# Output projection of a gated attention layer: tiles 8 and 9 as a fifth pair of seven half products

## The chip, the cores and the metric

The kernel runs on one core of one Trainium2 chip. Its time is the device time of one execution in microseconds (us); lower is better. The core has five engines with a queue of instructions each, which meet at semaphores: TensorE (PE; its weight loads are listed apart as PEld), VectorE (DVE), ScalarE (ACT), GpSimd (POOL) and SyncE (SP), which here issues the transfers.

## The reference, cut to what matters

With S = 2048 rows, D = 640 columns, 32 heads of 20 and F = 1536, all in fp32:

```
xn  = layernorm(x)
q, k, v = split(xn @ wqkv)                  # 32 heads of 20
o   = softmax(q . k[pos - 0,2,..,14]) @ v   # each position sees 8 positions, 2 apart
s   = o @ wo                                # the output projection
h   = (xn @ w_gate) * (xn @ w_up)
g   = silu(h @ w_down)
out = x + s * g
```

The change is in `s = o @ wo`, a product of 2048 x 640 by 640 x 640, and touches the preparation of w_down that runs beside it.

## The kernel before, in words

The rows lie in 16 tiles of 128 (s = 0 to 15). Each fp32 operand of a product is split into a high part, a rounded copy (ScalarE), and a low part, the rest (a subtraction on VectorE or GpSimd). A product is three sweeps of matmuls into one PSUM bank: high by high, high by low, low by high (`ALL3`). The stages run one after the other on TensorE: projections, gate and up; then the output projection; then the down projection, whose products of halves and sums of w_down's blocks need prepared weights ("down weights"). The whole order is written out by hand: each engine executes its instructions in the order in which the Python code issues them.

In the output projection, tiles 0 to 7 are taken in four pairs (p = 0 to 3, `pair_product`), each by seven products of halves after Strassen and Winograd, 320 columns wide: products 0 to 2 have 6 matmuls and products 3 to 6 have 9, as the fifth block of 128 rows of wo is added there in the plain way (`FIFTH`). Products 0, 2, 4 and 6 share bank A, 1 and 3 share bank C, 5 has bank B. ScalarE copies products 0 to 2 out (line 782), VectorE adds the kept ones to products 3, 4 and 5 (lines 785, 788, 790), ScalarE copies product 6 (line 793). Product 4 is read by VectorE before product 6 adds to the same bank.

The operands of a pair come in three parts, each with a high copy (`hi_pair`, line 754, ScalarE) and a low part (`lo_pair`, line 758, VectorE): part 0 is A11, A12 and the fifth block of the first tile, part 1 is S3, A22 and the fifth block of the second, part 2 is the sums S1, S2, S4. `turn_pair` transposes the two tiles (line 481) and forms the sums (734 to 737), after `load_pair` has brought them from DRAM. Product 0 of the next pair is issued ahead of product 6 of this one.

Tiles 8 to 15 go singly (`out_proj`): two halves of 15 matmuls each (line 96), their operand transposed by `turn_o` and split by `split_o`. The first half of tile 8 takes the place that product 0 of a next pair has.

Beside this run the twelve steps of the down weights, two for each k = 0 to 5: `wd_sums` issues their sums on VectorE (T1 and T2, lines 557 and 558; T3 and T4, lines 562 and 563), `wd_splits` their high copies on ScalarE (line 86) and low parts on GpSimd (line 87). T1 and T2 are tiles with the tag "lg", of which there are two buffers; T4 has one ("e"). In the first three pairs one step is taken, in pair 3 two (n = 2), beside each single tile one. In each pair the sums stand ahead of product 1, the splits behind product 4.

Buffers: the tag "wf" has four, two of which hold the first two blocks of wo during this stage. Odd pairs put part 2 into two "wf" buffers. The other parts lie in rows of down weight buffers that are not filled yet (`blocks(y, r, h, n)`: from row r of buffer y): `wd_kv["T4"]`, `wd_kv["B22"]`, `wd_big[0]` to `wd_big[3]`. A tile that is allocated when no buffer of its tag is free makes its first writer wait for the last reader of the old one.

Of the kernel before, what the change touches and what calls it, by code (L numbers as in the profile page):

```python
# [19 lines left out]
P = 128  # L20
S, D, F = 2048, 640, 1536
H, DH = 32, 20
W, DIL = 8, 2
NT = S // P
NE = NT // DIL
EXT = NE + W - 1
KD, KF = D // P, F // P
# [10 lines left out]
SCALE = DH ** -0.5  # L38
MASKED = -1e9 / SCALE
EPS = 1e-5  # L40
SP = NT // 2
PAIRS = range(0, W, 2)
PACE = 1.0

# [7 lines left out]
def kernel(  # L52
# [23 lines left out]
    def st(shape, tag, bufs, dt=F32):  # L76
        cnt[0] += 1
        return sb.tile(shape, dt, tag=tag, bufs=bufs, name=f"{tag}_{cnt[0]}")
# [5 lines left out]
    def split(eng, raw, hi, lo):  # L84

        nc.scalar.activation(hi, raw, AF.Copy)  # L86
        eng.tensor_sub(lo, raw, hi.bitcast(F32))  # L87
# [383 lines left out]
    def load_o(s, n, t):  # L471


        for b in range(NQ):
            nc.sync.dma_start(t[b * QB:(b + 1) * QB].rearrange("i n (q c) -> i (n q) c", c=QC),
                              o_scr[s // NE, b, s % NE:s % NE + n].rearrange("n (q i) c -> i (n q) c", i=QB))
        for i in range(n):
            o_t[s + i] = t[:, i]

    def turn(y, s):  # L480
        nc.vector.transpose(y.rearrange("p k (q i) -> p k q i", i=QB),
                            o_t.pop(s).rearrange("p (q k j) -> p k q j", q=NQ, j=QB))
# [3 lines left out]
    def turn_o(s):  # L486
        if not one_t:
            one_t.append(st([P, 2, KD, P], "ot", 2))
        y = one_t[0][:, s % 2]
        turn(y, s)  # L490
        return y

    def trans_o(s):
        split_o(s, turn_o(s))

    def split_o(s, y):
        if s == NT - 2:
            oT[s] = st([P, KD, P], "hs", 2, F32R), st([P, KD, P], "hs", 2, F32R)
        else:
            if s == SP:  # L500
                z = blocks(wd_kv["B22"], 4, 2, KD)
            else:
                z = st([P, 2, KD, P], *(("wf", 4) if s < NT - 2 else ("t", 2)), F32R)
            oT[s] = z[:, 0], z[:, 1]
        split(nc.vector, y, *oT[s])
# [3 lines left out]
    def out_proj(s, n):  # L509
        a = oT[s]  # L510
        if n == 0:
            y_t[s] = st([P, D], "hs" if s % 2 and s < NT - 4 else "gs", 2)
        c = slice(n * HALF, (n + 1) * HALF)
        p = pt([P, HALF], "q", 4)
        mm3(p, [([t[:, k, :] for t in a], [t[:, c] for t in wo_s[k]]) for k in range(KD)])
        nc.scalar.activation(y_t[s][:, c], p, AF.Copy)
        if n:
            oT.pop(s)
            nc.sync.dma_start(s_scr[s], y_t.pop(s))
# [7 lines left out]
    wd_big, wd_kv = [], {}  # L527
# [13 lines left out]
    def blocks(y, r, h, n):  # L541

        return y[:, r:].rearrange("p r i c -> p (r i c)")[:, :h * n * P].rearrange("p (h n c) -> p h n c", h=h, c=P)
# [63 lines left out]
    def hi_h(m):  # L607
        hT[m] = st([P, 2, KH, P], "wf", 4, F32R)
        nc.scalar.activation(hT[m][:, 0], h_raw[m // 7][H_IN[m % 7]], AF.Copy)  # L609
# [107 lines left out]
    def load_pair(p):  # L717
        if p:
            t = st([P, 3, D], "t", 2)
            load_o(2 * p, 2, t[:, 0:2])  # L720
            t = t.rearrange("p a c -> p (a c)")
        else:
            t = st([P, 2, D], "kv", 2)
            load_o(0, 2, t)
            t = t.rearrange("p a c -> p (a c)")
        pair_raw[p] = t[:, :3 * KS * P].rearrange("p (a c) -> p a c", c=P)

    def turn_pair(p):
        y = pair_y[p] = st([P, 2, KD, P], "ot", 2)
        for i in range(2):  # L730
            turn(y[:, i], 2 * p + i)
        s1, s2, s4 = (pair_raw[p][:, i * KS:(i + 1) * KS] for i in range(3))
        a11, a12, a21, a22 = (y[:, i, k:k + KS] for i in range(2) for k in (0, KS))
        nc.vector.tensor_add(s1, a21, a22)
        nc.vector.tensor_sub(s2, s1, a11)
        nc.vector.tensor_sub(s4, a12, s2)
        nc.vector.tensor_sub(a21, a11, a21)

    def hi_pair(p, part):

        if part == 2:
            if p % 2:
                z = [st([P, 2, KD, P], "wf", 4, F32R).rearrange("p a k c -> p (a k) c")[:, :3 * KS] for _ in range(2)]
            else:
                z = blocks(wd_kv["T4"], 2, 2, 3 * KS) if p else blocks(wd_big[0], 1, 2, 3 * KS)
                z = [z[:, 0], z[:, 1]]
            raw = pair_raw[p]
        else:
            y, r = (wd_big[3], 3) if p % 2 else (wd_kv["B22"], 2) if p else (wd_kv["T4"], 1)
            z = blocks(y, r, 2, 2 * KD)  # L750
            z = [z[:, i, part * KD:(part + 1) * KD] for i in range(2)]
            raw = pair_y[p][:, part]
        pair_z[p, part] = z, raw
        nc.scalar.activation(z[0], raw, AF.Copy)

    def lo_pair(p, part):
        z, raw = pair_z[p, part]
        nc.vector.tensor_sub(z[1], raw, z[0].bitcast(F32))
# [8 lines left out]
    def pair_product(p, j):  # L767
        place = "ACACABA"[j]
        new = j in (0, 1, 5)
        if new:  # L770
            bank[p, place] = pt([P, HALF], {"A": "q", "B": "g", "C": "u"}[place], {"A": 4, "B": 2, "C": 2}[place])
        b = bank[p, place]
        runs = [(pair_in(p, H_IN[j], k, i), w_part(W_IN[j], k, l)) for i, l in ALL3 for k in range(KS)]
        if j in FIFTH:
            name, c = FIFTH[j]
            runs += [(pair_in(p, name, 0, i), wo_t["W0-W1"][:, l] if c is None else wo_s[KD - 1][l][:, c:c + HALF])
                     for i, l in ALL3]
        for r, (y, w) in enumerate(runs):
            nc.tensor.matmul(b, y, w, start=new and r == 0, stop=r == len(runs) - 1, skip_group_check=True)  # L779
        kept, (ya, yb) = pair_k[0], y_t.setdefault((p, "y"), [None, None])  # L780
        if j < 3:
            nc.scalar.activation(kept[:, j], b, AF.Copy)
        elif j == 3:
            ya = y_t[p, "y"][0] = st([P, D], "gs", 2)
            nc.vector.tensor_add(ya[:, HALF:], kept[:, 2], b)
        elif j == 4:
            yb = y_t[p, "y"][1] = st([P, D], "hs", 2)
            nc.vector.tensor_add(yb[:, HALF:], kept[:, 1], b)
        elif j == 5:
            nc.vector.tensor_add(ya[:, :HALF], kept[:, 0], b)  # L790
            nc.sync.dma_start(s_scr[2 * p], ya)
        else:
            nc.scalar.activation(yb[:, :HALF], b, AF.Copy)
            nc.sync.dma_start(s_scr[2 * p + 1], yb)
# [180 lines left out]
    def wd_sums(n):  # L975
        for k, part in wd_steps[:n]:
            sum_wd(k, part)

    def wd_splits(n):
        for k, part in wd_steps[:n]:  # L980
            split_wd(k, part)
            if part and k + 2 < KH:
                load_wd(k + 2)
        del wd_steps[:n]

    pair_product(0, 0)
    for p in range(SP // 2):
        more = p + 1 < SP // 2
        n = (1, 1, 1, 2)[p]
        if not more:  # L990
            y8 = turn_o(SP)
        wd_sums(n)
        pair_product(p, 1)
        if more:
            hi_pair(p + 1, 0)
            lo_pair(p + 1, 0)
        else:
            split_o(SP, y8)
        pair_product(p, 2)
        if more:  # L1000
            hi_pair(p + 1, 2)
        pair_product(p, 3)
        if more:
            lo_pair(p + 1, 2)
            hi_pair(p + 1, 1)
        pair_product(p, 4)
        wd_splits(n)
        if more:
            lo_pair(p + 1, 1)
        pair_product(p, 5)  # L1010
        if p == 0:
            load_pair(3)
        elif p == 1:
            load_o(SP, 3, st([P, 3, D], "t", 2))
            turn_pair(3)
        elif p == 2:
            load_o(SP + 3, 3, st([P, 3, D], "t", 2))
        if more:
            pair_product(p + 1, 0)
        else:  # L1020
            out_proj(SP, 0)
        pair_product(p, 6)
    n_prod = 7 * NT // 2
    for s in range(SP, NT):
        if s + 1 < NT:
            trans_o(s + 1)
        if s == SP + 2:
            load_o(SP + 6, 2, st([P, 2, D], "t", 2))
        wd_sums(1)
        if s > SP:  # L1030
            out_proj(s, 0)
        out_proj(s, 1)
        wd_splits(1)
        if s == 12:
            load_h(0, ("A11", "A21", "A12"))
        elif s == 13:
            load_h(0, ("A22",))
        if s == 14:
            hi_h(0)
            lo_h(0)  # L1040
# [9 lines left out]
    for m in range(n_prod):  # L1050
        n, j = divmod(m, 7)
# [61 lines left out]
```

## Time and profile before

| | before |
|---|---|
| time, median of 3 runs | 781.13 us (781.04 to 781.26) |
| profiled execution | 781.13 us, span 779.2 us from first to last instruction |
| PE | busy 772.5 us, 4408 matmuls |
| DVE | busy 695.6 us, 731 instructions |
| ACT | busy 235.8 us, 536 instructions |
| POOL | busy 149.3 us, 114 instructions |
| output projection on PE | from 559.14 us to about 626.5 us of the span |

A row of a timeline gives the start in the span, the duration, the engine, the line, the operation, output and inputs by name, the shapes and the count; a bracket at its end gives the idle time before it and what ended it. Matmuls overlap, so the time that one costs in a row is the distance of starts. "Releasers" are inferred from semaphores.

### The profile page before, as it was taken

Reading aid. Unit: us, or ns where it says so; the run is one execution under the profiler, and the core shown is the slowest. Engines: PE = TensorE matmul, PEld = TensorE weight load, DVE = VectorE, ACT = ScalarE, POOL = GpSimd, SP = SyncE. Lnnn points to the kernel's source line nnn. Section 1 sums busy time; section 2 is a strip of 40 time slices with the busy share of each in tenths; the row PEclk is TensorE's granted clock in tenths of the full one; section 3 lists DMA queues with packets and bytes.
Section 4 is the critical chain, followed back from the end, with each engine's and each line's share of the span. In section 5 each row is a group of like instructions: output and inputs, shape, how many; then the busy total and the mean of one; then the engine's idle time right before and its main releaser. Section 6 shows DMA issues by size and latency. Waiting matters only on the chain.

```text
span 779.2 us, 11225 instructions
## 1 busy us (share of the span) xinstructions
PE 772.5 (99%) x4408; PEld 703.5 (90%) x4408; DVE 695.6 (89%) x731; ACT 235.8 (30%) x536; POOL 149.3 (19%) x114
## 2 busy tenths in 40 slices
PE   8999999999999999999999999999999999999997
PEld 6989888898989898989898989888899999999997
DVE  7999898999999999996999999999996787777775
ACT  4323312031112121311121212123455664444442
POOL 5200401022013101120204002042566710000000
PEclk9999999999999999999999999999999999999999
DMA  9562131331224122423123131354567674555533
GB/s 322 171 198 75 43 96 38 96 90 48 85 50 124 49 64 82 115 66 79 29 87 103 41 105 39 107 143 101 140 192 228 203 263 164 195 189 183 183 102 135
DMA packets 82236, 93.97 MB, mean 121 GB/s; under 512 B 23096, under 2 KB 63368, under 8 KB 82056
## 3 DMA queue, kind: packets, MB, share of 16 engines
q1 hardware_dynamic: 82184, 93.27, 38.8%
q8 instruction: 34, 0.56, 0.3%
q14 instruction: 18, 0.15, 0.1%
HBM read 55.84 MB, written 28.31 MB: 108 GB/s over the span
## 4 chain that ended last, share of the span: by engine, by line
PE 98%; DVE 1%; DMA 0%; issue 0%; ACT 0%; SPq 0%
PE q L307 27%; PE u L96 22%; PE g L96 22%; PE q L650 11%; PE u L650 5%; PE q L96 4%; PE g L650 3%; PE q L779 2%; PE u L779 1%; PE g L779 1%; DMA wraw<-in_wqkv 0%; DVE wqh L597 0%; SPq L136 0%; DVE wql L602 0%; DVE wqh L599 0%
## 5 line engine op out<-in xcount | busy, mean ns | idle before, releaser
L96 PE MATMUL g<-xc,wf 128*128 128x512 f32 (+1 forms) x735 | 176.2, 391 | 0.0
L96 PE MATMUL u<-xc,wf 128*128 128x512 f32 (+1 forms) x735 | 176.1, 390 | 0.0
L96 PEld LDWEIGHTS u<-xc,wf 128*128 128x128 f32 x735 | 135.9, 188 | 31.9
L96 PEld LDWEIGHTS g<-xc,wf 128*128 128x128 f32 x735 | 135.5, 188 | 30.8
L307 PE MATMUL q<-wqh,xc 128*128 128x300 f32 (+1 forms) x960 | 160.5, 311 | 0.4 <-ACT xc L232 0.3
L307 PEld LDWEIGHTS q<-wqh,xc 128*128 128x128 f32 x960 | 146.3, 188 | 2.7 <-ACT xc L232 0.8
L341 DVE TENSOR_TENSOR t<-q,kv 128x1600 f32<-128x1600 f32 (+1 forms) x48 | 96.9, 2019 | 8.2 <-ACT gs L410 7.2
L87 POOL TENSOR_TENSOR wf<-wraw,wf 128x256 fp32r<-128x256 f32 (+2 forms) x22 | 48.6, 2229 | 270.1 <-ACT wf L86 270.1
L362 DVE TENSOR_TENSOR t<-e,kv 128x1600 f32<-128x1600 f32 (+1 forms) x48 | 97.6, 2050 | 1.1
L344 DVE TENSOR_REDUCE lg<-t 128x80 f32<-128x1600 f32 (+1 forms) x48 | 92.6, 1929 | 1.1
L410 ACT ACTIVATE gs<-g 128x512 f32<-128x512 f32 x48 | 28.7, 597 | 204.2 <-PE g L96 193.2
L307 PE MATMUL q<-wql,xc 128*128 128x300 f32 (+1 forms) x480 | 86.2, 309 | 0.0
L370 DVE TENSOR_TENSOR t<-t,t 128x1600 f32<-128x1600 f32 (+1 forms) x36 | 76.5, 2124 | 1.0
L309 ACT ACTIVATE kv<-q 128x200 f32<-128x200 f32 (+1 forms) x96 | 33.4, 347 | 143.3 <-PE q L307 143.1
L307 PEld LDWEIGHTS q<-wql,xc 128*128 128x128 f32 x480 | 74.8, 188 | 0.0
L650 PE MATMUL q<-xc,wf 128*128 128x320 f32 x432 | 67.3, 309 | 0.1
L87 POOL TENSOR_TENSOR wql<-wraw,wqh 128x300 fp32r<-128x300 f32 (+4 forms) x14 | 33.3, 2400 | 168.0 <-ACT wqh L86 168.0
L650 PEld LDWEIGHTS q<-xc,wf 128*128 128x128 f32 x432 | 64.3, 188 | 0.4 <-ACT lg L627 0.4
L421 DVE TENSOR_TENSOR hs<-u,gs 128x512 f32<-128x512 f32 x47 | 32.1, 682 | 0.9 <-issue 0.9
L87 POOL TENSOR_TENSOR xc<-wraw,xc 128x320 fp32r<-128x320 f32 (+1 forms) x22 | 26.9, 1226 | 22.6 <-ACT xc L86 22.1
L310 ACT ACTIVATE q<-q 128x100 f32<-128x100 f32 (+1 forms) x96 | 24.6, 257 | 0.0
L613 DVE TENSOR_TENSOR wf<-t,wf 128x768 fp32r<-128x768 f32 x16 | 15.3, 957 | 8.5 <-ACT wf L609 7.8
(259 smaller groups left out, 909.1 us busy)
## 6 DMA issues: line engine op xcount, KB each, us to landing
h_scr<-hs SPq DMA_DIRECT2D x48, 256.0 KB, 2.3
wraw<-in_wgu SPq DMA_DIRECT2D x12, 640.0 KB, 4.6
t<-h_scr SPq DMA_DIRECT2D x8, 768.0 KB, 7.0
hs<-s_scr SPq DMA_DIRECT2D x16, 320.0 KB, 3.8
gs<-in_x SPq DMA_DIRECT2D x16, 320.0 KB, 4.1
out<-q SPq DMA_DIRECT2D x14, 320.0 KB, 2.6
wraw<-h_scr SPq DMA_DIRECT2D x11, 384.0 KB, 5.8
wraw<-in_wd SPq DMA_DIRECT2D x12, 320.0 KB, 3.6
```

The lines of the kernel that those rows point to most:

```text
L87: eng.tensor_sub(lo, raw, hi.bitcast(F32))
L96: nc.tensor.matmul(acc, a, b, start=first and n == 0, stop=last and n == len(runs) - 1)
L307: nc.tensor.matmul(p, xT[(r * NE + i) // TPC][a][:, k, t0:t0 + P], wq[g][b][:, k], start=n == 0, stop=n == len(runs) - 1, skip_group_check ...
L309: nc.scalar.activation(kv_t[u][:, :, W - 1 + i, :], p[:, c:].rearrange("p (a c) -> p a c", a=2), AF.Copy)
L341: nc.vector.tensor_mul(t, q.rearrange("p i c -> p (i c)").unsqueeze(1).to_broadcast([P, 2, NE * c]), places(0, j))
L344: nc.vector.tensor_reduce(out=lg[:, :, j:j + 2].rearrange("p n a -> p a n"), in_=heads(t), op=ALU.add, axis=AX.X)
L362: nc.vector.tensor_mul(heads(t), pw, heads(places(1, j)))
L370: nc.vector.tensor_add(acc, acc, t)
L410: nc.scalar.activation(gs, pp[0], AF.Copy)
L421: nc.vector.tensor_mul(hs, pp[1], gs)
L650: nc.tensor.matmul(p, y[:, i, k], wd_t[name][k][:, l], start=new and r == 0, stop=r == len(runs) - 1, skip_group_check=True)
L779: nc.tensor.matmul(b, y, w, start=new and r == 0, stop=r == len(runs) - 1, skip_group_check=True)
```

## The change

The border `SP` between pairs and single tiles moves from 8 to 10: tiles 8 and 9 become pair 4, tiles 10 to 15 stay single. Part 0 of pair 4 lies in rows 4 and 5 of `wd_kv["B22"]`, part 1 in rows 4 and 5 of `wd_big[2]`, tile 10's operand in rows 4 and 5 of `wd_big[3]`, part 2 in two "wf" buffers. Since those are the ones that pair 3's part 2 uses, `hi_pair(4, 2)` is issued behind product 3 of pair 3, not ahead of it. Pair 4 takes two steps of the down weights, as pair 3 does. The loads of tiles are regrouped: pair 4 after pair 1, tiles 10 to 12 after pair 2, tiles 13 to 15 after pair 3.

```diff
-SP = NT // 2
+SP = 10
...
             if s == SP:
-                z = blocks(wd_kv["B22"], 4, 2, KD)
+                z = blocks(wd_big[3], 4, 2, KD)
...
         if part == 2:
-            if p % 2:
+            if p % 2 or p > 3:
                 z = [st([P, 2, KD, P], "wf", 4, F32R).rearrange("p a k c -> p (a k) c")[:, :3 * KS] for _ in range(2)]
...
-            y, r = (wd_big[3], 3) if p % 2 else (wd_kv["B22"], 2) if p else (wd_kv["T4"], 1)
-            z = blocks(y, r, 2, 2 * KD)
-            z = [z[:, i, part * KD:(part + 1) * KD] for i in range(2)]
+            y, r = (wd_big[3], 3) if p % 2 else (wd_kv["T4"], 1) if p == 0 else (wd_kv["B22"], 2 if p == 2 else 4)
+            if p > 3 and part:
+                y, r = wd_big[2], 2
+            z = blocks(y, r + 2 * part, 2, KD)
+            z = [z[:, i] for i in range(2)]
...
-        n = (1, 1, 1, 2)[p]
+        n = (1, 1, 1, 2, 2)[p]
...
         pair_product(p, 2)
-        if more:
+        if more and p != 3:
             hi_pair(p + 1, 2)
         pair_product(p, 3)
         if more:
+            if p == 3:
+                hi_pair(p + 1, 2)
             lo_pair(p + 1, 2)
             hi_pair(p + 1, 1)
         pair_product(p, 4)
...
         elif p == 1:
-            load_o(SP, 3, st([P, 3, D], "t", 2))
+            load_pair(4)
             turn_pair(3)
         elif p == 2:
+            load_o(SP, 3, st([P, 3, D], "t", 2))
+            turn_pair(4)
+        elif p == 3:
             load_o(SP + 3, 3, st([P, 3, D], "t", 2))
...
-        if s == SP + 2:
-            load_o(SP + 6, 2, st([P, 2, D], "t", 2))
```

## The prediction

> **What bounds the kernel now.** I read the page first, for what ends last.
>
> ```profile
> span 779.2 us, 11225 instructions
> PE 772.5 (99%) x4408; PEld 703.5 (90%) x4408; DVE 695.6 (89%) x731; ACT 235.8 (30%) x536; POOL 149.3 (19%) x114
> PE 98%; DVE 1%; DMA 0%; issue 0%; ACT 0%; SPq 0%
> ```
>
> The last line is the chain that ended last: TensorE nearly everywhere, so a matmul taken out shortens the run by one pitch, and whatever holds TensorE lengthens it one for one. Next, the timeline of PE around the seam where the last pair (3) hands over to tile 8; the columns are start, duration, engine, line, shapes, count.
>
> ```profile
> 584.18 1.04 PE L779 MATMUL u<-xc,wf 128*128 128x320 f32 x6
> ...
> 587.27 1.04 PE L779 MATMUL q<-xc,xc 128*128 128x320 f32 x6
> ...
> 589.91 0.45 PE L96 MATMUL q<-wf,kv 128*128 128x320 f32 x2
> ...
> 592.35 1.11 PE L779 MATMUL q<-xc,xc 128*128 128x320 f32 x6
> ```
>
> These rows begin product 1 of pair 3, its product 4, the first half of tile 8, and product 6 of pair 3. Products 1 to 5 hold 6+6+9+9+9 = 39 matmuls and take 589.91 - 584.18 = 5.73 us, a pitch of 0.147 us. Tile 8's 15 would take 2.20 at that pitch and took 592.35 - 589.91 = 2.44: only 0.24 us lost. TensorE is all but unstalled there. But the other queues show how little is missing. VectorE, same stretch and the pair before:
>
> ```profile
> 574.81 1.56 DVE L481 STREAM_TRANSPOSE ot<-t 128x640 f32<-128x640 f32 x2
> ...
> 578.36 0.48 DVE L557 TENSOR_TENSOR lg<-wraw 128x320 f32<-128x320 f32 x1
> 578.93 0.49 DVE L558 TENSOR_TENSOR lg<-wraw,lg 128x320 f32<-128x320 f32 x1
> 579.34 0.82 DVE L758 TENSOR_TENSOR xc<-ot,xc 128x640 fp32r<-128x640 f32 x1
> 580.08 0.48 DVE L785 TENSOR_TENSOR gs<-o,u 128x320 f32<-128x320 f32 x1
> 580.48 0.95 DVE L758 TENSOR_TENSOR wf<-t,wf 128x768 fp32r<-128x768 f32 x1
> 581.35 0.48 DVE L788 TENSOR_TENSOR hs<-o,q 128x320 f32<-128x320 f32 x1
> ...
> 583.17 0.83 DVE L481 STREAM_TRANSPOSE ot<-t 128x640 f32<-128x640 f32 x1
> 583.93 0.85 DVE L562 TENSOR_TENSOR wraw<-wraw 128x320 f32<-128x320 f32 x1
> ...
> 585.11 0.48 DVE L557 TENSOR_TENSOR lg<-wraw 128x320 f32<-128x320 f32 x1
> 588.91 1.15 DVE L558 TENSOR_TENSOR lg<-wraw,lg 128x320 f32<-128x320 f32 x1 [3.32 <-POOL xc L87]
> 589.98 1.49 DVE L87 TENSOR_TENSOR kv<-ot,kv 128x640 fp32r<-128x640 f32 x1
> 591.39 0.47 DVE L785 TENSOR_TENSOR gs<-o,u 128x320 f32<-128x320 f32 x1
> 591.79 0.47 DVE L788 TENSOR_TENSOR hs<-o,q 128x320 f32<-128x320 f32 x1
> ```
>
> The row at 588.91 carries the whole prediction. Pair 3 takes two down weight steps at once (n = 2): the second half of k = 1 and the first half of k = 2. The sums of both stand ahead of the splits of both. T2 of k = 2 (line 558) goes into one of two "lg" buffers, and the one it gets still holds T2 of k = 1, which is split only later in the pair. So VectorE stands still for 3.32 us, until GpSimd has read the old T2. Everything behind it on VectorE waits too: the low part of tile 8, then the sums of products 3 and 4. Here that was nearly free, since fifteen matmuls of tile 8 stood between product 5 and product 6.
>
> What releases T2 are copies on ScalarE and, behind them, subtractions on GpSimd:
>
> ```profile
> 578.68 0.85 ACT L754 ACTIVATE wf<-t 128x768 fp32r<-128x768 f32 x1
> 579.41 0.74 ACT L754 ACTIVATE xc<-ot 128x640 fp32r<-128x640 f32 x1
> 580.04 0.47 ACT L86 ACTIVATE xc<-wraw 128x320 fp32r<-128x320 f32 x1
> ...
> 586.60 0.47 ACT L86 ACTIVATE xc<-wraw 128x320 fp32r<-128x320 f32 x1
> 586.96 0.47 ACT L86 ACTIVATE xc<-lg 128x320 fp32r<-128x320 f32 x1
> ```
>
> ```profile
> 587.99 0.89 POOL L87 TENSOR_TENSOR xc<-lg,xc 128x320 fp32r<-128x320 f32 x1
> ...
> 590.74 1.46 POOL L87 TENSOR_TENSOR xc<-wraw,xc 128x320 fp32r<-128x320 f32 x1
> ...
> 592.99 0.88 POOL L87 TENSOR_TENSOR xc<-lg,xc 128x320 fp32r<-128x320 f32 x1
> ```
>
> The splits of pair 3 start on ScalarE at 586.60; 2.31 us later VectorE is let go.
>
> **What the change takes off TensorE.** Tiles 8 and 9 singly: 2 x 2 halves x 15 = 60 matmuls. A pair: 3 products of 6 and 4 of 9 = 54. Six fewer at 0.147: -0.88 us.
>
> **What it adds beside TensorE, at no cost.** Four sums of 256 columns, 768 more columns of copy and low part, three evacuations moved from ScalarE to VectorE: some 4 us of VectorE, in two pairs where it idled 3.32 us in one wait. turn_pair(4) comes at 583.17, after pair 2; pair 3's ran from 574.81 to 578.36, 3.55 us, so it ends at 586.72; the three sums before T2 took 585.11 - 583.93 + 0.41 = 1.59 (0.41 being the step from 578.93 to 579.34), so VectorE reaches T2 at 588.31, inside the wait. Without that cover it would cost the difference, and that is in the second rival. The transfers keep their distance: pair 4 is loaded one pair before its transposition, as pair 3 was, tile 10 likewise, and no load moves ahead of the down weights on SP's queue. The down weight steps keep their places against tiles 10 to 15, so the seam to the last stage just shifts. The corners hold data that is used up before they are filled; a wait on them ends with pair 2's product 6, before 584.18.
>
> **What it does to pair 3: the cost.** Pair 3 now has a successor that is a pair, and still n = 2. Two things follow.
>
> First, the splits start later. ScalarE's queue gets hi_pair(4, 2) and hi_pair(4, 1) ahead of them. hi_pair(4, 2) writes two "wf" buffers, and the other two hold wo, so it needs those of pair 3's S1, S2, S4, read until product 3 ends, 587.27 plus the overlap of a matmul's own 0.3 us: 587.5. The two copies then take 0.73 and 0.63 (steps 578.68 to 579.41 to 580.04). The splits start at 588.86 instead of 586.60: +2.26. So T2 starts at 588.91 + 2.26 = 591.17.
>
> Second, what is queued behind T2 is now urgent. Product 0 of pair 4 starts at 589.91 and has six matmuls, of which the last two need lo_pair(4, 0), behind T2. Product 6 of pair 3 adds to the bank that VectorE reads in product 4's sum, behind that and behind lo_pair(4, 2), which the change also put there. TensorE, which goes in order, would reach product 6 at 589.91 + 6 x 0.147 = 590.79. VectorE gets there so: T2 591.17; the low part 1.07 later (588.91 to 589.98), 592.24; product 3's sum 1.41 later (589.98 to 591.39), 593.65; lo_pair(4, 2) 0.40 later, 594.05; product 4's sum after a step for 768 columns, 0.87 undisturbed (580.48 to 581.35) and, as the low part beside GpSimd went from 0.74 to 1.41, up to 1.5; I take 1.0, as GpSimd is in the middle of one operation there, so 595.05; its end 0.47 later and 0.09 to the matmul (592.26 to 592.35): 595.61. TensorE loses 595.61 - 590.79 = 4.8 us, in two pieces: some 3.2 us before the last two matmuls of product 0 and some 1.6 us before product 6.
>
> The ends: with every step undisturbed, as in pair 2, the way from T2's start to the matmul is 581.35 + 0.48 - 578.93 + 0.09 = 2.99 in place of 4.44, a loss of 3.4. With the longest (1.5 for the 768 columns, and T2 and the low part 0.1 longer each), 5.5. GpSimd works through its seven operations in that very stretch, and T2 and the low part stand against them as they did before, so I stay near the upper part.
>
> [...]
>
> **Pair 4** then stands where pair 3 stood: n = 2, and a single tile as successor. Its splits come 2.42 us after product 1 starts (584.18 to 586.60), that is at about 599.3, and GpSimd is through with pair 3's at 592.99 + 0.88 + 2.26 = 596.1. So it pays the 0.24 us that pair 3 paid, no more.
>
> **Sum.** -0.88 + 4.8 = +3.9 us. The profiled execution took 781.13 us (1.93 around its span of 779.2), which is the median too: 781.13 + 3.95 = 785.1 us, span 783.1. Ends: 783.6 and 785.7.
>
> **Rivals.** (1) *The splits are not later*: ScalarE has both copies behind it in time, and T2 starts at 588.91 as now. What is behind T2 is urgent all the same: 588.91 + 4.44 = 593.35, a loss of 2.6, 782.8 us. For it: only that two other "wf" buffers might be free; against: four buffers are all there are, two with wo and two with pair 3's S1, S2 and S4. 1 in 10.
>
> (2) *Not slower: the wait on T2 is gone*, because its buffer comes out differently or T2 of k = 1 is read early. Then T2 starts at 588.31 and 2.99 later product 6 may start: 591.30, 0.5 lost, 781.13 - 0.88 + 0.5 = 780.75. It decides at T2's start: only before about 587.8 would TensorE see nothing. Against it: the wait stands in this trace, and neither the tag nor n at pair 3 changes. 0.07.
>
> (3) *TensorE comes back slowly*. After its start, ten matmuls of 300 columns took a pitch of 0.231 (7.17 to 9.48), ten later ones 0.138 (19.86 to 21.24):
>
> ```profile
> 7.17 2.48 PE L307 MATMUL q<-wqh,xc 128*128 128x300 f32 x10 [0.18 <-ACT xc L232]
> 9.48 0.44 PE L307 MATMUL q<-wql,xc 128*128 128x300 f32 x2
> ...
> 19.86 1.54 PE L307 MATMUL q<-wqh,xc 128*128 128x300 f32 x10
> 21.24 0.85 PE L307 MATMUL q<-wql,xc 128*128 128x300 f32 x5
> ```
>
> ```profile
> core 0: us, PE busy (x) PEld busy (x) DVE busy (x) ACT busy (x) POOL busy (x), PEclk, DMA share, GB/s
> 5.00:10.00 5.00, 4.45 (x20) 2.67 (x19) 4.61 (x16) 2.83 (x8) 3.23 (x4) 1.00 0.99 319
> 583.00:592.00 9.00, 9.00 (x62) 8.75 (x61) 5.68 (x9) 4.78 (x12) 6.29 (x7) 1.00 0.91 251
> ```
>
> The granted clock (PEclk) reads 1.00 in both stretches, so the trace doesn't say whether the clock made the early ones slow. Here TensorE would idle 4.8 of 5.1 us, which no stretch of this trace after its start shows. If twelve matmuls after it ran at the slow pitch, 12 x 0.093 = 1.1 us more: 786.2. Against it: the first gap is about 3.2 us and two matmuls break the idleness. 0.15. [...]
>
> **How the numbers follow.** Forecast 0.65, rivals 0.10, 0.07 and 0.15; 0.03 is left for what I haven't seen. The range reaches from rival (1), 782.8, to the upper end with the slow pace, 785.7 + 1.1 = 786.8; outside lie rival (2) and the rest, 1 in 10. A measurement tells 0.2%, 1.6 us, from no change. The six matmuls are 0.11%, so even a perfect hiding is "the same": faster 0.01, same 0.08, slower 0.91.
>
> **What would show it.** In the profile after: line 558 in pair 3 with an idle time of about 2.9 us before it, released by GpSimd; the ScalarE copy into "wf" starting right after product 3; two gaps of PE between product 0 of pair 4 and product 6 of pair 3, of about 3.2 and 1.6 us, released by VectorE; no such gap in pair 4; 54 matmuls for it at 0.147. If T2 waits but PE shows no gap, I have the order of VectorE wrong; if the copies are done before 587, the first step is wrong; if TensorE's pitch behind the gaps is above 0.147, rival (3).

## The result, and the profile after

The changed kernel takes 786.81 us (786.08 to 787.34, six runs) against 781.27 us before, a ratio of 1.0067 (95% interval 1.0057 to 1.0077): slower by some 5.5 us. The profiled execution took 786.95 us, its span is 785.0 us.

The timeline of PE in the changed kernel shows where. Columns as before: start, duration, engine, line, operation, shapes, count, and in the bracket the idle time ahead of the row and what ended it.

```profile
559.03 1.04 PE L781 MATMUL q<-wf,kv 128*128 128x320 f32 x6
...
586.24 0.31 PE L781 MATMUL u<-wql,wf 128*128 128x320 f32 x1
...
589.77 0.75 PE L781 MATMUL q<-wf,kv 128*128 128x320 f32 x4
592.89 0.90 PE L781 MATMUL q<-wf,kv 128*128 128x320 f32 x2 [2.38 <-DVE kv L760]
594.84 1.97 PE L781 MATMUL q<-xc,xc 128*128 128x320 f32 x6 [1.04 <-DVE hs L790]
...
599.00 1.26 PE L781 MATMUL q<-xc,wf 128*128 128x320 f32 x6
600.11 0.31 PE L781 MATMUL u<-wqh,wf 128*128 128x320 f32 x1
```

The first row is the first product of the output projection, the second one of the nine matmuls of product 3 of pair 3, which is needed further down. Product 0 of pair 4 starts at 589.77, four of its matmuls run, and then TensorE stands for 592.89 - (589.77 + 4 x 0.147) = 2.5 us and again for 594.84 - (592.89 + 2 x 0.147) = 1.7 us, both times until VectorE is through: 4.2 us. (The brackets give less, 2.38 and 1.04 us: they count from the end of the last matmul, this sum from the time when the next one would have started; and the two matmuls before the second gap run slowly, which the next lines explain.) What follows is a second loss. The 21 matmuls from 594.84 to 600.11 take 5.27 us, a pitch of 0.25; at 0.147 they'd take 3.09. That is 2.2 us more. The stretches of 0.5 us name the reason (PEclk, the granted clock, is the number before the last two):

```profile
592.00:592.50 0.50, 0.00 (x0) 0.00 (x0) 0.50 (x1) 0.00 (x0) 0.50 (x2) 1.00 0.11 41
592.50:593.00 0.50, 0.10 (x1) 0.11 (x1) 0.50 (x2) 0.00 (x0) 0.50 (x1) 0.66 0.06 26
...
599.00:599.50 0.50, 0.50 (x3) 0.50 (x3) 0.00 (x0) 0.20 (x1) 0.00 (x0) 0.51 1.12 306
599.50:600.00 0.50, 0.50 (x5) 0.50 (x5) 0.00 (x0) 0.50 (x2) 0.00 (x0) 1.00 1.16 232
```

The clock goes from 1.00 to 0.50 at about 592.7, 2.3 us into the first gap, and comes back at 599.5, 6.8 us later. VectorE's and ScalarE's timelines show what the gaps wait for, and one row of GpSimd what VectorE waits for:

```profile
587.03 0.49 DVE L557 TENSOR_TENSOR lg<-wraw 128x320 f32<-128x320 f32 x1
590.31 1.14 DVE L558 TENSOR_TENSOR lg<-wraw,lg 128x320 f32<-128x320 f32 x1 [2.80 <-POOL xc L87]
591.37 1.47 DVE L760 TENSOR_TENSOR kv<-ot,kv 128x640 fp32r<-128x640 f32 x1
592.77 0.47 DVE L787 TENSOR_TENSOR gs<-o,u 128x320 f32<-128x320 f32 x1
593.16 1.22 DVE L760 TENSOR_TENSOR wf<-t,wf 128x768 fp32r<-128x768 f32 x1
594.31 0.47 DVE L790 TENSOR_TENSOR hs<-o,q 128x320 f32<-128x320 f32 x1
```

```profile
586.64 0.85 ACT L756 ACTIVATE wf<-t 128x768 fp32r<-128x768 f32 x1
587.39 0.72 ACT L756 ACTIVATE xc<-ot 128x640 fp32r<-128x640 f32 x1
588.02 0.46 ACT L86 ACTIVATE xc<-wraw 128x320 fp32r<-128x320 f32 x1
```

```profile
589.39 0.88 POOL L87 TENSOR_TENSOR xc<-lg,xc 128x320 fp32r<-128x320 f32 x1
```

It is the row that the prediction rested on: T2 of k = 2 waits until 590.31, when GpSimd has read the old T2 (589.39 + 0.88), and low part, sum, low part, sum follow it in order.

The last stage's first product starts here:

```profile
632.28 2.80 PE L650 MATMUL q<-xc,wf 128*128 128x320 f32 x18
```

Before, the first product of the output projection and that row stood at:

```profile
559.14 1.04 PE L779 MATMUL q<-wf,kv 128*128 128x320 f32 x6
...
626.56 2.80 PE L650 MATMUL q<-xc,wf 128*128 128x320 f32 x18
```

So the stretch between grew from 67.42 to 73.25 us, by 5.83: -0.88 for six matmuls, +4.19 for the gaps, +2.18 for the clock, and 0.34 of rest, nearly all of it in the last five tiles (150 matmuls from 610.07 to 632.28, a pitch of 0.148; before, 0.146). This stretch, "the stage" below, leaves out the start of the program, which differs by up to 0.9 us between the profiled executions (the first product starts at 558.94 to 559.84); the last stage itself takes the same 145.54 us from its first to its last product in both (626.56 to 772.10, 632.28 to 777.82).

### The profile page after: what moved, and what is told of

It is laid out like the page before. It is cut to its first block, busy times and chain, and to the rows that moved or that the text cites. A ratio compares the mean times of both kernels' runs of the same rounds, so it can differ in the third digit from the quotient of the medians.

```text
span 785.0 us, 11228 instructions
## 1 busy us (share of the span) xinstructions
PE 774.8 (99%) x4402; PEld 704.9 (90%) x4402; DVE 698.2 (89%) x739; ACT 237.1 (30%) x537; POOL 150.5 (19%) x114
## 4 chain that ended last, share of the span: by engine, by line
PE 95%; issue 1%; DMA 1%; DVE 1%; POOL 1%; SPq 0%; ACT 0%; DVEq 0%; POOLq 0%; ACTq 0%
PE q L307 27%; PE u L96 21%; PE g L96 21%; PE q L650 10%; PE u L650 5%; PE q L96 3%; PE g L650 3%; PE q L781 2%; PE u L781 1%; DMA wraw<-in_wqkv 1%; POOL xc L87 1%; PE g L781 1%; DMA s_scr<-hs 0%; SPq L107 0%; DVE wqh L597 0%
```

## The experiments

Theory A: the double step of pair 3, which straddles two k with two T buffers, holds VectorE in front of a pair's urgent work, and idleness lowers TensorE's clock. Theory B: the fifth pair itself is too much for VectorE and ScalarE.

| kernel | median, us | ratio to before (95%) | stage in the profiled execution, us |
|---|---|---|---|
| changed | 786.81 | 1.0067 (1.0057 to 1.0077) | 73.25 |
| double step in pair 2 | 783.00 | 1.0018 (1.0009 to 1.0028) | 69.40 |
| double step in pair 1 | 786.98 | 1.0070 (1.0057 to 1.0084) | 72.54 |
| three lg buffers | 780.97 and 780.76 | 0.9991 (0.9982 to 1.0001), 0.9993 (0.9984 to 1.0002) | 66.64 and 66.97 |
| both gaps filled | 785.08 | 1.0046 (1.0030 to 1.0061) | 71.30 |
| first gap filled | 786.37 | 1.0063 (1.0049 to 1.0077) | 71.28 |
| second gap filled | 786.47 | 1.0070 (1.0056 to 1.0083) | 72.40 |
| splits ahead | 785.23 | 1.0044 (1.0030 to 1.0058) | 72.32 |
| three lg, double step in pair 1 | 782.13 | 1.0012 (1.0003 to 1.0021) | 68.17 |
| before, three lg | 781.17 | 0.9998 (0.9990 to 1.0007) | 67.33 |
| late step | 782.44 | 1.0016 (1.0008 to 1.0025) | 66.62 |
| three lg, late step | 784.40 | 1.0036 (1.0022 to 1.0050) | 66.63 |

**Three lg buffers: the wait by itself.** Nothing is moved; only the tag gets one more buffer (the attention and the last stage use the same tag, and get it too).

```diff
-            v["T1"], v["T2"] = st([P, HALF], "lg", 2), st([P, HALF], "lg", 2)
+            v["T1"], v["T2"] = st([P, HALF], "lg", 3), st([P, HALF], "lg", 3)
```

> The changed kernel with three buffers for the tag lg instead of two, and the same instructions in the same order. Theory A: T2 of k = 2 takes the third buffer in pair 3, VectorE reaches it at about 587.5 us of the span and doesn't stop; low part, product 3's sum, the second low part and product 4's sum follow in 3.0 us, so product 6 of pair 3 finds its bank at about 591 and loses at most 0.5 us; no slow clock; 780.4 to 781.2 us. Theory B: as order and work are unchanged, 785 us or more.

VectorE's timeline of this kernel, and PE's:

```profile
587.86 0.48 DVE L557 TENSOR_TENSOR lg<-wraw 128x320 f32<-128x320 f32 x1
588.43 0.49 DVE L558 TENSOR_TENSOR lg<-wraw,lg 128x320 f32<-128x320 f32 x1
588.84 0.82 DVE L760 TENSOR_TENSOR kv<-ot,kv 128x640 fp32r<-128x640 f32 x1
...
591.14 0.47 DVE L790 TENSOR_TENSOR hs<-o,q 128x320 f32<-128x320 f32 x1
```

```profile
590.60 1.04 PE L781 MATMUL q<-wf,kv 128*128 128x320 f32 x6
591.67 1.15 PE L781 MATMUL q<-xc,xc 128*128 128x320 f32 x6
```

T2 follows T1 at once, and from product 0 to product 6 of the seam pass 1.07 us for six matmuls of 0.88: 0.2 us lost in place of 4.2, and no slow clock (PEclk 1.00 from 591 to 600). This undoes the whole loss without touching the fifth pair's work, so theory B as the main cause falls, and A's first half is shown. It is within the range that was expected.

**The double step elsewhere.** In pair 1 it straddles k = 0 and 1; in pair 2 it holds both halves of k = 1.

```diff
-        n = (1, 1, 1, 2, 2)[p]
+        n = (1, 2, 1, 1, 2)[p]        # in pair 1
+        n = (1, 1, 2, 1, 2)[p]        # in pair 2
```

> The changed kernel with (1, 2, 1, 1, 2) down weight steps: the double step moves from pair 3 to pair 1, where it again holds the second half of one k and the first of the next (k = 0 and 1), ahead of another pair. Pair 3 keeps the late copy of part 2. Theory A (a double step that straddles two k, with two T buffers, in front of a pair): idle time at line 558 in pair 1, two gaps of PE between product 0 of pair 2 and product 6 of pair 1, together about 4 us, the clock at half behind them for 2.2 us of loss, and none of it at pair 3: 786 to 787.5 us. Theory B (it is pair 4's own work, or the late copy, at pair 3): the gaps stay at the seam of pairs 3 and 4 and none comes at pair 1.

The stall went along, to the seam of pairs 1 and 2, and nothing stayed at pairs 3 and 4 (VectorE first, then PE):

```profile
574.83 1.14 DVE L558 TENSOR_TENSOR lg<-wraw,lg 128x320 f32<-128x320 f32 x1 [4.65 <-POOL xc L87]
```

```profile
577.41 0.56 PE L781 MATMUL q<-wf,kv 128*128 128x320 f32 x2 [2.19 <-DVE kv L760]
579.36 1.14 PE L781 MATMUL q<-xc,xc 128*128 128x320 f32 x6 [1.38 <-DVE hs L790]
...
595.93 1.04 PE L781 MATMUL q<-wf,kv 128*128 128x320 f32 x6
596.81 1.04 PE L781 MATMUL q<-xc,xc 128*128 128x320 f32 x6
```

At 595.93 stands the seam of pairs 3 and 4, late copy and all, with 0.88 us for six matmuls: not a tenth lost.

> The five pairs take (1, 1, 2, 1, 2) down weight steps instead of (1, 1, 1, 2, 2): the double step moves from pair 3 to pair 2, where it holds both halves of k = 1, so that no T2 is overwritten inside the pair. Theory A (the wait on the T2 buffer in pair 3, and TensorE's slow clock behind the gap that it makes, cost all): no idle time at line 558 in pair 3, no gap of PE between product 0 of pair 4 and product 6 of pair 3, clock 1.00; the six matmuls remain, less the 0.3 us of slower pitch in the last five tiles, so 780.4 to 780.8 us. Theory B (the fifth pair itself is too much for VectorE and ScalarE: more copies, more low parts, the late copy of part 2): the gaps stay at 2 us or more and the time above 783 us.

Here A was only half right. No T2 waits, but product 6 does, for 1.5 us (VectorE, then PE):

```profile
585.90 0.80 DVE L734 TENSOR_TENSOR t<-ot 128x256 f32<-128x256 f32 x1
586.74 0.98 DVE L735 TENSOR_TENSOR t<-t,ot 128x256 f32<-128x256 f32 x1
587.76 0.99 DVE L736 TENSOR_TENSOR t<-ot,t 128x256 f32<-128x256 f32 x1
...
589.58 0.49 DVE L558 TENSOR_TENSOR lg<-wraw,lg 128x320 f32<-128x320 f32 x1
```

```profile
592.96 1.15 PE L781 MATMUL q<-xc,xc 128*128 128x320 f32 x6 [1.53 <-DVE hs L790]
```

Pair 2's two splits give GpSimd more to do while VectorE forms the sums of pair 4 (busy for 5.64 of the 8 us from 583 to 591, against 3.75 with three lg buffers), and these take 0.80 to 0.99 us instead of the 0.42 that they take in the changed kernel, where GpSimd is idle. The three together are 1.5 us longer than undisturbed, and product 6 is late by about as much. So the rows speak for theory B as a second, smaller cause, with VectorE short of time at these seams. No run takes this cause away by itself, so its size isn't shown.

**The clock.** Matmuls that nobody reads go into the gaps, on operands that are ready.

```diff
+        at, fills = {(4, 0): (2 * KS, 15), (3, 6): (0, 8)}.get((p, j), (None, 0))
...
+            if r == at:
...
+                for _ in range(fills):
+                    nc.tensor.matmul(spare[0], wo_s[KD - 1][0][:, :P], wo_s[KD - 1][0][:, HALF:], ...)
```

> The changed kernel with 23 extra matmuls that nobody reads: 15 ahead of the last two matmuls of product 0 of pair 4, 8 ahead of product 6 of pair 3. At 0.147 us they take 2.2 and 1.2 us, less than the two gaps (2.5 and 1.7 us), so that they take nobody's place and only keep TensorE busy. If the slow pitch behind the gaps comes from idleness: granted clock 1.00 from 590 to 600, 21 matmuls in 3.1 us instead of 5.3, time 2.2 us under the changed kernel, about 784.6 us. If it comes from something else (memory, the operands in the corners): pitch as slow as before, 786.8 us or more.

PE with both gaps filled:

```profile
590.36 2.36 PE L788 MATMUL g<-q 128*128 128x320 f32 x15
592.94 0.56 PE L790 MATMUL q<-wf,kv 128*128 128x320 f32 x2 [0.22 <-DVE kv L760]
593.34 1.34 PE L788 MATMUL g<-q 128*128 128x320 f32 x8
594.88 1.16 PE L790 MATMUL q<-xc,xc 128*128 128x320 f32 x6 [0.21 <-DVE hs L799]
...
598.08 0.31 PE L790 MATMUL u<-wqh,wf 128*128 128x320 f32 x1
```

Product 6 starts where it did (594.88 against 594.84), and the 21 matmuls behind it now take 598.08 - 594.88 = 3.20 us instead of 5.27, with PEclk at 1.00 from 590 to 600. 23 more matmuls make the kernel 1.7 us faster by the medians (2.2 were expected). That the slow pitch comes from idleness is shown.

The next two ask which gap does it.

> The changed kernel with the 15 unread matmuls in the first gap alone; the second, 1.7 us, stays empty. [...]

> The changed kernel with the 8 unread matmuls in the second gap alone; the first, 2.5 us, stays empty. The clock fell inside this first gap in the changed kernel, before the second began, so it falls here too, in all or most executions: 786 to 787 us, mean clock 0.995 to 0.998; and the 8 matmuls at the slow pitch take 2.1 us, up to 0.5 us more than the gap. If only both gaps together make it fall, 785.1 us.

With the first gap filled and the second left (1.38 us by the bracket; PE below), the profiled execution kept the clock (PEclk 1.00 from 589 to 602) and took 785.32 us; the three others took 786.4 with a mean clock of 0.997. The kernel before read 0.997 or less in only two of its 65 executions beside these runs. So such a gap can be enough, and whether it is changes from execution to execution.

```profile
593.18 0.56 PE L790 MATMUL q<-wf,kv 128*128 128x320 f32 x2 [0.20 <-DVE kv L760]
595.13 1.15 PE L790 MATMUL q<-xc,xc 128*128 128x320 f32 x6 [1.38 <-DVE hs L799]
```

With the second gap filled and the first left (2.38 us), three of four executions took 786.5 to 787.9 us at a mean clock of 0.994 to 0.996, as expected. The fourth took 785.77 us at 0.998, which leaves open whether its clock fell: the second run with three lg buffers also has 0.998, at 780.66 us, below its own median, and so has the double step in pair 1, with the clock low for 3.4 us in the stage. In the profiled one the clock fell only after the gap had ended:

```profile
593.27 0.56 PE L790 MATMUL q<-wf,kv 128*128 128x320 f32 x2 [2.38 <-DVE kv L760]
593.67 1.73 PE L788 MATMUL g<-q 128*128 128x320 f32 x8
```

```profile
593.00:594.00 1.00, 0.73 (x5) 0.73 (x6) 1.00 (x3) 0.00 (x0) 1.00 (x2) 1.00 0.05 20
594.00:595.00 1.00, 1.00 (x7) 0.99 (x6) 1.00 (x2) 0.00 (x0) 1.00 (x1) 0.70 0.00 0
```

The expectation that it falls inside the gap was wrong for this execution.

The traces hold one thing more. The clock was low for 6.82 us in the changed kernel (592.66 to 599.48), for 6.83 with the splits ahead (592.98 to 599.81), and for 3.4 both with the second gap filled (594.4 to 597.8) and with the double step in pair 1 (580.4 to 583.9). In the last 3.4 us before it fell TensorE was idle for 2.1 us in the changed kernel, 2.3 with the second gap filled, 1.6 with the splits ahead and 1.8 with the double step in pair 1. But in this last kernel it was idle for 1.8 us also in the 3.4 us that end at 577.03, and the clock stayed at 1.00 there. So neither the length of a gap nor this sum tells alone whether the clock falls, and what does isn't shown.

**Splits ahead of the copies.** `wd_splits(n)` of pair 3 moves from behind product 4 to behind product 2.

```diff
+        if p == 3:
+            wd_splits(n)
         pair_product(p, 3)
...
-        wd_splits(n)
+        if p != 3:
+            wd_splits(n)
```

> In the changed kernel, pair 3's splits of the down weights are issued behind product 2 instead of product 4, that is ahead of the two copies for pair 4 on ScalarE. The splits start at about 586.5 instead of 588.0, T2 of k = 2 at about 588.8 instead of 590.3. Theory A: the first gap of PE shrinks from 2.5 to about 1.0 us, both together from 4.2 to about 2.7. If a gap of 2.4 us is what the clock needs to fall, it stays at 1.00 now and the time is 781.3 - 0.9 + 2.7 + 0.3 = 783.4 us; if less is enough, it falls all the same and the time is about 785.5 us. Theory B: hardly any change from 786.8 us.

```profile
592.03 0.56 PE L781 MATMUL q<-wf,kv 128*128 128x320 f32 x2 [1.24 <-DVE kv L760]
593.97 1.97 PE L781 MATMUL q<-xc,xc 128*128 128x320 f32 x6 [1.39 <-DVE hs L790]
```

The first gap shrank from 2.5 to 592.03 - 590.04 - 4 x 0.147 = 1.4 us, the second stayed at 1.65: 3.05 instead of the expected 2.7. Of seven executions three kept a mean clock of 0.999 (783.4 to 784.3 us) and four had 0.996 or 0.997 (785.2 to 786.3): both of the expected outcomes, in one kernel. In the profiled one the clock fell at 592.98, and its two gaps are 1.24 and 1.39 us by the brackets. ScalarE's order is thus a part of the stall, about a quarter of it, and taking it away doesn't pay for the wait.

**Towards a faster version.** These move the double step as well.

> Three buffers for the tag lg and (1, 2, 1, 1, 2) steps. No T2 waits any more; the double step lies in pair 1, where VectorE idled 1.5 us, and pair 3, where turn_pair(4) fills VectorE, has two sums instead of four. Theory A: no gap of PE above 0.1 us from product 0 of pair 0 to the last stage, which comes 66.3 to 66.6 us after it (before: 67.4, changed: 73.3, three buffers with the double step in pair 3: 66.6); 780.2 to 780.8 us. If VectorE's load is what counts (second cause, seen as 1.5 us of waiting in the run with the double step in pair 2), pair 1 loses 0.5 us or more and the time is 781 us or above.

A miss: 0.77 us at the seam of pairs 2 and 3 and 0.25 at the next, both until line 790 on VectorE. VectorE's rows for pair 3's sums are again 0.79 to 1.10 us long. By the order of the code GpSimd works through two steps (pair 1's) beside them, which no row here shows.

> The kernel before with three buffers for the tag lg. Its wait of 3.3 us at line 558 in pair 3 goes, and with it the 0.24 us that tile 8 lost: the last stage comes 67.2 instead of 67.4 us after the first product, 781.0 us. That is the measure of what the third buffer gives without the fifth pair; what the fifth pair gives by itself is the distance from here to the changed kernel with three buffers, 0.6 to 0.9 us.

The kernel before lost its wait and its stage went from 67.42 to 67.33 us; the time is the same. Without a pair behind it the wait cost nothing that can be measured.

> The changed kernel with (1, 1, 1, 1, 2) steps and two lg buffers: pair 3 has one step, pair 4's two are both halves of k = 2, and the twelfth step comes beside tile 15. No T2 is overwritten inside a pair. Theory A: no wait at line 558 in pair 3, gaps of PE at most 0.3 us, the last stage 66.4 to 66.8 us after the first product. The last step's four subtractions on GpSimd then end about 4.5 us later than now, 3 us into the last stage; its third product is the first that needs one of them, 5.3 us in, so nothing waits: 780.3 to 780.9 us. If VectorE or ScalarE have no room for the last step at tile 15, the last stage's first copies come late and PE waits there, 781 us or more.

A miss in the time. The stage is as short as expected, 66.62 us, but the last stage pays: its third product waited 1.6 us for ScalarE's copy at line 627. I took that for the lg buffers, which that copy also uses, and tried a third one:

> Three buffers for the tag lg and (1, 1, 1, 1, 2) steps, the twelfth beside tile 15. With two buffers the output projection lost nothing (66.6 us to the last stage), but the last stage's first results, which also go into lg, waited 1.6 us for the last T2. If that is why that kernel took 782.4 us, a third buffer takes the wait away: the last stage as long as before (145.5 us from its first to its last product) and 780.6 to 780.9 us. If instead the late splits themselves (ScalarE, GpSimd) hold the last stage, 782 us or more.

The wait stayed as it was:

```profile
633.41 2.91 PE L650 MATMUL q<-xc,wf 128*128 128x320 f32 x18 [1.59 <-ACT lg L627]
```

So it wasn't the buffer. VectorE's and ScalarE's rows of this kernel:

```profile
627.53 1.52 DVE L599 TENSOR_TENSOR wqh<-wqh,wraw 128x768 f32<-128x768 f32 x1
...
630.53 1.62 DVE L602 TENSOR_TENSOR wql<-o,wqh 128x768 f32<-128x768 f32 x1
...
633.61 0.95 DVE L605 TENSOR_TENSOR ot<-wraw,ot 128x768 f32<-128x768 f32 x1
```

```profile
632.19 0.85 ACT L609 ACTIVATE wf<-wql 128x768 fp32r<-128x768 f32 x1 [2.26 <-DVE wql L602]
632.94 0.42 ACT L627 ACTIVATE lg<-q 128x320 f32<-128x320 f32 x1
```

As long as GpSimd splits the late step (626.75 to 632.87), VectorE's sums take 1.5 to 1.6 us instead of 0.95; S4 (line 602) is late, ScalarE's copy of it stands ahead of line 627, and TensorE waits for that. This is read from the rows; no run moves GpSimd's work away. Three of its five executions also had a mean clock of 0.997 and took 784.4 to 784.7 us, two, the profiled one among them, kept 1.00 at 782.4 and 782.5. The gap of 1.59 us is the likely reason in those three, but no trace shows them; with two buffers and a gap of 1.60 us the mean clock was 0.998 or more in all eleven executions.

> The changed kernel with three lg buffers once more, in more rounds and beside the kernel with the late step: whether the fifth pair, freed of its wait, is faster than the kernel before. By TensorE's times from the first product of this stage to the last stage, 66.6 against 67.4 us: 780.5 against 781.2 us, a ratio of 0.9990. A rival: a start that differs from run to run by half a microsecond hides it, and the interval holds 1.

The changed kernel with three lg buffers is the fastest of all: 780.97 against 781.32 and 780.76 against 781.15 us on two chips, 0.35 and 0.39 us less. Each interval holds 1, so that it beats the kernel before isn't shown by the times; the stage, in one profiled execution each, says 0.5 to 0.8 us.

## Why the prediction was right, and where it was not

Direction and mechanism were right: T2's wait in pair 3, the work queued behind it, two gaps at the seam, no more than about 0.25 us at the next one; 786.81 us lies at the very edge of the range (786.8). That it lies no further out is partly luck: the edge stands for gaps of 5.5 us and 1.1 us of slow pitch, and what came was 4.2 and 2.2. By steps:

- *Six matmuls, -0.88 us.* Seen only where the stall is gone: with three lg buffers in both, the stage is 66.64 or 66.97 us with the fifth pair and 67.33 without. Of the 0.88, 0.2 is lost at the seam, which leaves the 0.69 of the first of these; the second has the slower pitch of the last bullet besides.
- *The splits come 2.26 us later.* They came 1.56 later: 588.02 against 586.60, with all of this kernel 0.14 us early by then. The copy into "wf" started at 586.64, not at 587.5 less 0.14. The step that failed: I let product 3 hold both buffers to its end. The copy needs only the one with the high parts, and in the order of the sweeps the fourth of the nine matmuls is the last to read it: 586.24 to 586.55. The copy even started before the sixth, the last to read the low parts, would have ended (586.54 + 0.31).
- *The way from T2 to product 6, 4.44 us.* It took 594.84 - 590.31 = 4.53. The step for 768 columns was 1.15 (593.16 to 594.31), where I took 1.0, an estimate. Two operations of GpSimd ran beside the step, from 592.12 to 593.57 and from 593.52 to 595.10. One ran beside the 0.87 that I called undisturbed as well, but it started at 580.59, after VectorE's row at 580.48.
- *The gaps, 4.8 us.* 4.2, of 2.5 and 1.7 instead of 3.2 and 1.6.
- *The clock, rival (3).* This is the step that was mis-sized. I gave it 0.15 and 1.1 us; it came in all six timed executions (mean clock 0.995 to 0.997) and cost 2.2 us in the profiled one. I held it unlikely because the first gap would be about 3.2 us and two matmuls break the idleness; that this would be too little was my estimate, and no row of the kernel before showed it. The gap was shorter still, and the clock fell from 1.00 to 0.50 when 2.3 us of it had passed; with the splits ahead it fell in an execution whose longest gap was 1.39 us by the bracket. With 4.2 and 2.2 the sum is -0.88 + 4.2 + 2.2 = +5.5, and 786.81 - 781.27 = 5.5 was measured. That they agree so well is in part chance: the sum is that of the profiled execution, which took 5.8 us more than the one before, with 0.3 from the next bullet, and three of the six, at a mean clock of 0.997, took only 786.1 to 786.8.
- *The slower pitch of the last five tiles*, 0.148 against 0.146, 0.3 us, was not foreseen. It isn't the change's: the kernel with three lg buffers, the same in both its runs, has these 150 matmuls in 21.88 us on one chip (604.60 to 626.48) and in 22.22 on another (603.69 to 625.91). What makes it stays open.

## What to carry to other kernels

When a step is moved into a queue that already holds a wait, list what now stands behind that wait and who needs it: a wait of 3 us that had been free cost 4 us when a pair followed it, and one more buffer undid it. Price a stall of TensorE with its clock: here gaps of 1.4 us by the bracket could cost another 1 us, the two of the changed kernel cost 2.2, and unread matmuls in the gaps saved that. Before moving work of GpSimd, look at the VectorE operations beside it: here, with one of GpSimd's running at its start, a low part of 768 columns took 1.22 us instead of 0.95 (593.16 in the changed kernel) and a sum of 256 columns 1.40 instead of 0.42 (560.90), while the sums that read a product from its bank stayed at 0.47 (592.77, 594.31).

## What the runs showed of the hardware

TensorE's granted clock halved, 1.00 to 0.50, behind gaps of 1.24 to 2.38 us, and the length of a gap alone didn't decide it. By the brackets, and judged by mean clock and time where there is no trace: two gaps of 2.38 and 1.04 us (changed kernel) did it in all six executions, one of 2.38 (second gap filled) in three of four and perhaps the fourth, two of 2.19 and 1.38 (double step in pair 1) in the profiled one of four, two of 1.24 and 1.39 (splits ahead) in four of seven, one of 1.38 (first gap filled) in three of four, one of 1.59 (three lg, late step) in three of five. But one of 1.60 (late step) did it in none of eleven, and one of 1.53 (double step in pair 2) in none of ten. The clock could fall more than 1 us after TensorE was busy again (the gap ended at 593.27, the clock fell at 594.4), and in four traces it stayed low for 3.4 or 6.8 us.

A copy into the buffer of a stationary operand started at 586.64, 0.1 us after the last matmul that reads this buffer had ended, while the same product went on with other operands; which buffer it is, is read from the order in the code. VectorE's 768-column operations took 0.95 to 0.96 us with GpSimd idle (changed kernel, 633.86 to 642.99), and 0.95 where one of GpSimd's started after theirs (580.34 and 580.45); where one was running when theirs began, they took 1.22 to 1.64 (changed kernel, 593.16 and 632.19; three lg, late step, 628.97).
